# The logits products of a part in two portions of 24, in a mixture-of-experts kernel

## The chip, the cores and the metric

The kernel runs on one core of a Trainium2 chip. A core has five engines that work side by side: TensorE (PE, matrix products; its weight loads are listed apart as PEld), VectorE (DVE), ScalarE (ACT), GpSimd (POOL) and SyncE (SP, which here only issues transfers). Each works through its own instructions in order. TensorE writes its results to PSUM, a small memory of 8 banks, from which VectorE and ScalarE fetch them; all else is held in SBUF.

The metric is the device time of one execution in microseconds, lower being better. A profile is one more execution, recorded instruction by instruction.

## What is computed

A short convolution along the sequence, then a layer of eight experts, of which each token uses one. The reference, cut to what matters:

```python
B, S, D, E, F = 8, 3584, 192, 8, 1024          # everything in float32

# convolution: 8 heads of 24 channels, 7 taps each, softmax over the taps
out = np.einsum('hk,bskhg->bshg', w, x_unf)

# experts
logits = np.einsum('bsd,de->bse', x, w_gate)
local_gate = 1.0 / (1.0 + np.exp(-np.einsum('bsd,de->bse', x, w_local).squeeze(-1)))
for b in range(B):
    prev_e = -1
    for s in range(S):
        fresh_e = int(np.argmax(logits[b, s]))
        if s == 0 or local_gate[b, s] < 0.5:
            e = fresh_e
        else:
            e = prev_e if prev_e >= 0 else fresh_e
        prev_e = e
        ls = logits[b, s] - logits[b, s].max()
        p = np.exp(ls)
        p /= p.sum() + 1e-09
        h = np.maximum(x[b, s] @ w1[e], 0.0)
        out[b, s] = p[e] * (h @ w2[e])
```

A token takes the expert with the largest logit, or, if its local gate is open, the expert of the token before it. The eight logits and the local gate of a token are nine products over 192 channels. They are small beside the two products with w1 and w2, but nothing of a token's expert is known before them.

## The kernel before

The 28,672 tokens are cut into 16 parts of 1792. A part goes through three stages.

- *Convolution.* In the first two parts it is done as products of TensorE (`wide`). In the other 14, `conv` does it: the first tap of a head on ScalarE (L378), six more on VectorE (L388).
- *Route.* `route` (L603) finds each token's expert and its place among that expert's tokens. It begins with `logits` (L566): VectorE transposes the part in squares of 32 by 32 into the tile z (L572); TensorE forms the logits (L582); ScalarE copies them out of PSUM (L587, tile ls); VectorE transposes them back (L590, lq) and puts them in order (L598, lt). Some hundred short VectorE operations follow; they end in the places of the tokens (posi, L747) and in tables of which rows and whose weights a block needs (L847). `put` (L770) has GpSimd scatter the rows to their places in a DRAM buffer, slots.
- *Experts.* A block is one unit (n = 1) or two units (n = 2) of 128 tokens of one expert. SyncE loads its weights (wb, L906) and rows (xg, L913) ahead of time. For each block TensorE does three things: `hidden` (L952) forms the 1024 hidden values in two halves, `for two in range(2)`, of twelve products each (L963), and ScalarE applies relu (L968); `turn` (L930) transposes the rows of the block that comes next (L360, into the PSUM tile xps, then copied to xT by L947 and L949); `output` (L973) forms the result (L980, 16 products for each unit), which ScalarE (L988) and VectorE (L992) scale and add, and GpSimd scatters to the output (L996).

After the start, 55 blocks of one unit and 87 blocks of two are run: 35 of one unit, the 87 of two, then 20 of one. The convolution and the route of the later parts are worked into the first 96 of them.

The order of all instructions is the order in which the program writes them. `conv` and `route` are generators that give a time for each operation, and `step(time)` (L1037) takes operations from them until that time is used up: from the route first, from the convolution after. A route yields "hop" where it has to wait for another engine; then the rest of that call of `step` goes to the convolution, and the route goes on in the next call. `step` is called between turn and output (L1150), within output before line 992 (L990), and after output (L1152). The products of `logits` thus land where the call of `step` stands that reaches them.

The logits products are short. z holds four groups of tokens that lie on different rows, and the weights of the gate have 32 columns, so that one product uses 64 rows and 32 columns of TensorE and streams 128 values: six blocks of 32 channels, by four groups j, by two halves of the rows make 48 products. In float32, each appears in the profile as two products with a weight load each. The long products beside them (L963, L980) use 64 rows and all 128 columns.

PSUM holds one tile xps (two banks), four tiles hps, of which a half of `hidden` takes two, and two tiles yps, which an output takes. The sums of the logits are two of the hps tiles (L577).

Of the kernel before, what the change touches and what calls it, by code (L numbers as in the profile page):

```python
# [8 lines left out]
F32 = mybir.dt.float32  # L9
# [8 lines left out]
P = 128  # L18
# [19 lines left out]
BT = 2 * UT  # L38
# [25 lines left out]
Q = 32  # L64
DQ = D // Q
TQ = (NT + 3) // 4
# [15 lines left out]
def kernel(  # L82
# [10 lines left out]
    nc = tc.nc  # L93
# [11 lines left out]
    xps_p = ctx.enter_context(tc.tile_pool(name="xps_p", bufs=1, space=PSUM))  # L105
    hps_p = ctx.enter_context(tc.tile_pool(name="hps_p", bufs=4, space=PSUM))
# [77 lines left out]
    wgb, wgq = wg[:, :3, :], wg[:, 3:, :]  # L184
# [5 lines left out]
    def z_tile():  # L190
        return yt.tile([P, 3 * NH * TB + NB * DR], F32, name="z")
# [119 lines left out]
    rows = cst.tile([Q, 2, Q], F32, name="rows")  # L311
# [42 lines left out]
    def halves():  # L354
        return [(half, slice(half * DR, (half + 1) * DR)) for half in range(2)]
# [210 lines left out]
    def logits(g, y_sb):  # L566

        nc.gpsimd.tensor_copy(y_sb[:, :, Y0 + D:IX], y_sb[:, :, Y0 + P:Y0 + D])  # L568
        z = z_tile()[:, :NT * D].rearrange("p (t d) -> p t d", d=D)
        for t in range(0, NT, TQ):  # L570
            u = min(t + TQ, NT)
            nc.vector.transpose(z[:, t:u, :], y_sb[:, t:u, Y0:Y0 + D])  # L572
            yield 0.2 * (u - t)
        yield "hop"


        lps = [hps_p.tile([P, TQ * Q], F32, name="hps") for half in range(2)]  # L577
        begin = [min(TQ * j, NT - TQ) for j in range(4)]
        for b in range(DQ):
            for j in range(4):  # L580
                for half, rows in halves():
                    nc.tensor.matmul(lps[half][Q * j:Q * j + Q, :], lhsT=wgq[rows, b, :],  # L582
                                     rhs=z[rows, begin[j]:begin[j] + TQ, b * Q:(b + 1) * Q],
                                     start=(b == 0), stop=(b == DQ - 1))
        ls = sm.tile([P, 2, TQ * Q], F32, name="ls", bufs=1)
        for half in range(2):
            nc.scalar.copy(ls[:, half, :], lps[half])  # L587
        yield "hop"
        lq = sm.tile([P, 2 * TQ, Q], F32, name="lq", bufs=1)
        nc.vector.transpose(lq.rearrange("p t e -> p (t e)"), ls.rearrange("p h x -> p (h x)"))  # L590
        yield 0.4
        lt = sm.tile([P, NT + 2, E + 1], F32, name="lt")
        for r in range(4):
            for j in range(4):
                t, u = TQ * j, min(TQ * (j + 1), NT)
                at = r // 2 * TQ + t - begin[j]
                e0 = r % 2 * (E + 1)
                nc.vector.tensor_copy(lt[Q * r:Q * r + Q, t:u, :],  # L598
                                      lq[Q * j:Q * j + Q, at:at + u - t, e0:e0 + E + 1])
                yield 0.12  # L600
        return lt
# [168 lines left out]
    def put(behind=None):  # L770


        if not to_put:
            return
        g, rows, to = to_put.pop(0)
        nc.gpsimd.nop()
        ins = nc.gpsimd.indirect_dma_start(  # L777
            out=slots[:, :], in_=rows, in_offset=None,
            out_offset=bass.IndirectOffsetOnAxis(ap=to, axis=0)).ins
        if behind is not None:  # L780
            tc.add_manual_dep(ins, behind.ins.name, SYNC, reason="scatters apart")
        if puts:
            tc.declare_no_dep(ins, group="puts", reason="slots of their own")
        if g:
            tc.declare_no_dep(ins, group="gets", reason="those slots were full before")
        puts.append((g, ins))
        tc.add_to_no_dep_group("puts", ins)
        tc.add_to_no_dep_group(f"puts{g}", ins)
# [163 lines left out]
    def hidden(n, wb, xT, shares=(1, 1)):  # L952
        hT = hp.tile([P, FK, BT], F32, name="hT")
        w = slice(0, n * P)


        for two in range(2):
            hps = [hps_p.tile([P, 2, BT], F32, name="hps") for half in range(2)]
            for d in range(KD):
                for j in range(2):  # L960
                    f0 = (d * 4 + two * 2 + j) * P
                    for half, rows in halves():
                        nc.tensor.matmul(hps[half][:, j, w], lhsT=wb[rows, f0:f0 + P],  # L963
                                         rhs=xT[rows, d, w], start=(d == 0 and j == 0),
                                         stop=(d == KD - 1), skip_group_check=True)
            for half in range(2):
                m = half * 4 + two * 2
                relu = nc.scalar.activation(hT[:, m:m + 2, w], hps[half][:, :, w], Act.Relu)  # L968
            for _ in range(shares[two]):
                put(relu)  # L970
        return hT

    def output(n, wb, xg, hT):  # L973

        yps = [yps_p.tile([P, 512], F32, name="yps") for half in range(2)]
        for m4 in ([0, 1, 4, 5], [2, 3, 6, 7]):
            for k in range(n):
                for m in m4:
                    for half, rows in halves():
                        nc.tensor.matmul(yps[half][:, k * D:(k + 1) * D],  # L980
                                         lhsT=hT[rows, m, k * P:(k + 1) * P],
                                         rhs=wb[rows, WA + m * D:WA + (m + 1) * D],
                                         start=(m == 0 and k == 0), stop=(m == FK - 1),
                                         skip_group_check=True)
        o_sb = op.tile([P, KT, D], F32, name="o_sb")
        y = [[yps[half][:, k * D:(k + 1) * D] for half in range(2)] for k in range(n)]
        for k in range(n):
            nc.scalar.activation(o_sb[:, k, :], y[k][0], Act.Copy, scale=xg[:, k, 0:1])  # L988

        step(1.2)  # L990
        for k in range(n):
            nc.vector.scalar_tensor_tensor(o_sb[:, k, :], y[k][1], xg[:, k, 0:1], o_sb[:, k, :],  # L992
                                           Alu.mult, Alu.add)

            nc.gpsimd.nop()
            sent = nc.gpsimd.indirect_dma_start(  # L996
                out=out, in_=o_sb[:, k, :], in_offset=None,
                out_offset=bass.IndirectOffsetOnAxis(ap=xg.bitcast(I32)[:, k, IX:], axis=0),
                bounds_check=N - 1, oob_is_err=False)
            tc.declare_no_dep(sent.ins, group="sent", reason="each token has one slot")  # L1000
            tc.add_to_no_dep_group("sent", sent.ins)
# [1 line left out]

    LEAD = 2
    LATE = 3
    st = {"block": 0, "conv": 1, "cgen": None, "route": 1, "rgen": None, "routed": 1}

    def start_conv():
        g = st["conv"] + 1

        free = not any(p[0] <= g - 3 for p in to_put)
        if (st["cgen"] is None and g < NPART and g <= st["route"] + LEAD and free
                and (g != 3 or g in x_in and st["block"] > LATE + 2)):
            st["conv"] = g
            st["cgen"] = conv(g, x_in.pop(g))
            next(st["cgen"])
# [7 lines left out]
    def start_route():  # L1024
        done = st["conv"] - (st["cgen"] is not None)
        if st["rgen"] is None and st["route"] < done:
            st["route"] += 1
            st["rgen"] = route(st["route"])
# [8 lines left out]
    def step(time):  # L1037

        start_route()
        start_conv()  # L1040
        go = st["rgen"] is not None
        while time > 0:
            c = route_op() if go else conv_op()
            if c is None:
                if not go:
                    break
                go = False
            elif c == "hop":
                go = False
            elif c == "placed":  # L1050
                pass
            else:
                time -= c
# [85 lines left out]
    for i, (_, n, _, _) in enumerate(blocks):  # L1139
        st["block"] = i  # L1140
        ensure(i)
        weights(i + AHEAD)
        if i == LATE:
            x_in[3] = load_x(3)
        hT = hidden(n, wbs[i], xT, (1, 1) if i else (0, 0))
        if i + 1 < len(blocks):
            xT, copied = turn(blocks[i + 1][1], xgs[i + 1])
            if len(to_put) > NT // 2 and n == KT:
                put(copied)
        step(2.1 if n == 1 else 4.2)  # L1150
        output(n, wbs.pop(i), xgs.pop(i), hT)
        step(1.3 if n == 1 else 3.0)  # L1152

# [79 lines left out]
```

## Time and profile before

| | us |
|---|---|
| median of three runs | 1340.1 |
| lowest and highest | 1337.61 and 1342.41 |
| the profiled execution's own time | 1340.85 |
| its span, from the first to the last instruction | 1339.1 |

Groups of instructions of one line (busy time, and mean duration of one):

| line | engine | what | count | busy us | mean ns |
|---|---|---|---|---|---|
| L980 | PE | output products | 7328 | 647.0 | 326 |
| L963 | PE | hidden products | 6816 | 634.5 | 336 |
| L360 | PE | transposes of the rows | 916 | 60.3 | 221 |
| L388 | DVE | convolution | 672 | 376.1 | 569 |
| L968 | ACT | relu | 568 | 262.1 | 512 |
| L587 | ACT | copies of the logits | 28 | 6.1 | 269 |

Products on TensorE overlap, so that a group's busy time is less than its count by its mean. "Idle time before", where a line of a profile gives it, is the time for which that engine had nothing to do just ahead of these instructions, and the name behind the arrow is what ended it; "issue" is written where the engine waited for nothing that the profile shows. In an order of time, the columns are the start, the length, the engine and the line, the operation, what is written and read, and the number of instructions, with the idle time before them in brackets. In a table by stretches, each row is a stretch of the span: its length, each engine's busy time with the number of instructions, the clock granted to TensorE, the share of the DMA engines, and GB/s.

### The profile page before, as it was taken

The page shows a single profiled execution, that of the slowest core. Times are in us where ns is not written, and L with a number is a line of the kernel's source. Part 1 is how long each engine was busy: PE and PEld are TensorE (multiplying, and loading weights), DVE is VectorE, ACT ScalarE, POOL GpSimd, SP SyncE. Part 2 cuts the span into 40 slices and gives each one's busy share as a digit, 9 for nine tenths or more (in the row PEclk, how much of TensorE's full clock was granted, in tenths as well). Part 3 has the DMA queues.
Part 4 walks back from the last instruction along what each step waited for, and adds up shares of the span by engine and source line. Part 5 has one row for each costly group of instructions (what it writes and reads, how often), then busy time and mean ns, then how long its engine had stood idle before and what let it go on. Part 6 is the DMA issues. An engine that isn't in the chain of part 4 may idle for free. (4 is left out here: it accounts for less than half of the span.)

```text
span 1339.1 us, 41274 instructions
## 1 busy us (share of the span) xinstructions
PE 1315.2 (98%) x16682; PEld 1264.3 (94%) x16682; DVE 778.6 (58%) x2434; ACT 583.9 (44%) x1431; POOL 492.8 (37%) x538
## 2 busy tenths in 40 slices
PE   8899999999999999999999999999999999999997
PEld 7898999899999999999999999999999999999997
DVE  5878887877777777868786878786520000000000
ACT  5244544444444444444444444444334333334443
POOL 4455443534343434343434343434344211121111
PEclk9899999999999999999999999999999999999999
DMA  4799999977575857675767675756566655556893
GB/s 180 262 357 406 376 352 356 365 281 276 192 287 189 295 197 286 209 274 208 274 209 274 208 281 207 288 204 234 206 234 230 207 185 184 190 192 235 322 332 124
DMA packets 67298, 340.36 MB, mean 254 GB/s; under 512 B 12576, under 2 KB 23191, under 8 KB 47650
## 3 DMA queue, kind: packets, MB, share of 16 engines
q1 hardware_dynamic: 44784, 284.88, 59.2%
q0 software_dynamic: 22320, 52.82, 10.4%
q8 instruction: 133, 2.18, 0.6%
q14 instruction: 59, 0.48, 0.1%
q10 hardware_dynamic: 2, 0.00, 0.0%
HBM read 284.73 MB, written 53.41 MB: 253 GB/s over the span
## 5 line engine op out<-in xcount | busy, mean ns | idle before, releaser
L980 PE MATMUL yps<-wb,hT 64*128 64x192 f32 x7328 | 647.0, 326 | 8.2 <-ACT hT L968 5.3
L963 PE MATMUL hps<-xT,wb 64*128 64x256 f32 (+1 forms) x6816 | 634.5, 336 | 1.6 <-issue 1.2
L980 PEld LDWEIGHTS yps<-wb,hT 64*128 64x128 f32 x7328 | 603.7, 187 | 19.6 <-ACT hT L968 10.8
L963 PEld LDWEIGHTS hps<-xT,wb 64*128 64x128 f32 x6816 | 585.1, 187 | 28.7 <-issue 3.2
L996 POOL DMA_INDIRECT out_dram<-o_sb,xg x229 | 232.4, 1015 | 608.6 <-DVE o_sb L992 540.1
L968 ACT ACTIVATE hT<-hps 128x512 f32<-128x512 f32 (+1 forms) x568 | 262.1, 512 | 393.1 <-PE hps L963 271.6
L388 DVE SCALAR_TENSOR_TENSOR y_sb<-x_sb,c,y_sb 128x336 f32<-128x336 f32 x672 | 376.1, 569 | 20.1 <-ACT y_sb L378 2.0
L992 DVE SCALAR_TENSOR_TENSOR o_sb<-yps,xg,o_sb 128x192 f32<-128x192 f32 x229 | 87.5, 413 | 475.7 <-ACT o_sb L988 468.5
L777 POOL DMA_INDIRECT slots<-y_sb,posi x228 | 228.0, 1000 | 207.4 <-ACT hT L968 81.6
L988 ACT ACTIVATE o_sb<-yps,xg 128x192 f32<-128x192 f32 x229 | 86.9, 418 | 305.4 <-PE yps L980 299.7
L949 ACT COPY xT<-xps 64x256 f32<-64x256 f32 (+1 forms) x284 | 92.4, 325 | 7.0
L947 ACT COPY xT<-xps 128x512 f32<-128x512 f32 (+1 forms) x142 | 72.2, 509 | 5.9 <-PE xps L360 2.9
L360 PEld LDWEIGHTS xps<-ident,xg 64*128 64x128 f32 x916 | 60.2, 139 | 5.2
L378 ACT ACTIVATE y_sb<-x_sb,c 128x336 f32<-128x336 f32 x112 | 63.7, 581 | 1.0
L360 PE MATMUL xps<-ident,xg 64*128 64x64 f32 x916 | 60.3, 221 | 0.0
L572 DVE STREAM_TRANSPOSE z<-y_sb 128x768 f32<-128x768 f32 (+1 forms) x56 | 45.4, 852 | 0.4
L598 DVE COPY lt<-lq 32x36 f32<-32x36 f32 x224 | 41.0, 183 | 3.5
L582 PE MATMUL hps<-z,wg 64*32 64x128 f32 x1344 | 24.1, 272 | 0.7 <-issue 0.5
L582 PEld LDWEIGHTS hps<-z,wg 64*32 64x32 f32 x1344 | 19.0, 105 | 3.1 <-issue 2.3
L556 PE MATMUL yps<-y_sb 112*128 112x194 f32 x64 | 13.8, 377 | 1.8 <-DVE y_sb L550 1.8
L556 PEld LDWEIGHTS yps<-y_sb 112*128 112x128 f32 x64 | 12.5, 220 | 2.6 <-DVE y_sb L550 2.0
L568 POOL COPY y_sb<-y_sb 128x896 f32<-128x896 f32 x14 | 13.4, 954 | 0.0
(240 smaller groups left out, 384.0 us busy)
## 6 DMA issues: line engine op xcount, KB each, us to landing
wb<-in_w_dram SPq DMA_DIRECT2D x138, 1536.0 KB
x_sb<-in_x_dram SPq DMA_DIRECT2D x14, 1920.0 KB
xg<-slots SPq DMA_DIRECT2D x87, 259.0 KB
xg<-slots SPq DMA_DIRECT2D x53, 129.5 KB
wb<-in_w_dram SPq DMA_DIRECT2D x12, 512.0 KB
out_dram<-o_sb,xg POOLq DMA_INDIRECT x229
slots<-y_sb,posi POOLq DMA_INDIRECT x228
x_sb<-in_xb_dram SPq DMA_DIRECT2D x4, 768.0 KB
```

Source lines behind the costliest of these rows:

```text
L360: nc.tensor.transpose(to, src[rows], identity=ident[rows, rows])
L378: nc.scalar.activation(cols(h), chans(h, 0), Act.Copy, scale=c[:, h, 0:1])
L388: nc.vector.scalar_tensor_tensor(cols(h), chans(h, k), c[:, h, k:k + 1], cols(h), Alu.mult, Alu.add)
L777: ins = nc.gpsimd.indirect_dma_start(out=slots[:, :], in_=rows, in_offset=None, out_offset=bass.IndirectOffsetOnAxis(ap=to, axis=0)).ins
L947: nc.scalar.copy(first, by)
L949: copied = nc.scalar.copy(to[rows, :, 2], at[(DR, 0)[half]:(P, DR)[half], :, 0])
L963: nc.tensor.matmul(hps[half][:, j, w], lhsT=wb[rows, f0:f0 + P], rhs=xT[rows, d, w], start=(d == 0 and j == 0), stop=(d == KD - 1), skip_g ...
L968: relu = nc.scalar.activation(hT[:, m:m + 2, w], hps[half][:, :, w], Act.Relu)
L980: nc.tensor.matmul(yps[half][:, k * D:(k + 1) * D], lhsT=hT[rows, m, k * P:(k + 1) * P], rhs=wb[rows, WA + m * D:WA + (m + 1) * D], start= ...
L988: nc.scalar.activation(o_sb[:, k, :], y[k][0], Act.Copy, scale=xg[:, k, 0:1])
L992: nc.vector.scalar_tensor_tensor(o_sb[:, k, :], y[k][1], xg[:, k, 0:1], o_sb[:, k, :], Alu.mult, Alu.add)
L996: sent = nc.gpsimd.indirect_dma_start(out=out, in_=o_sb[:, k, :], in_offset=None, out_offset=bass.IndirectOffsetOnAxis(ap=xg.bitcast(I32)[ ...
```

## The change

The loop over the six blocks of 32 channels is cut into two portions of three, 24 products each, and the copies to ls follow the second. How the portions are kept apart depends on which call of `step` reaches them. A new flag, "ahead", is set during the call between turn and output.

- With the flag set, the sums are two hps tiles as before, now asked for with the full 512 columns of a bank. The first portion is written; a "hop" leaves it to the next call, which is the one within output, behind all products of line 980, to write the second portion and the copies; another "hop" follows.
- Without it, the sums are the two banks of an xps tile. The first portion is written where the step stands, behind an output. The second is left in st["amid"], and `hidden` of the next block calls it after its first half: behind the relus and puts of that half, ahead of the other twelve products.

In the order of instructions, 11 of the 14 parts have a whole output between the portions (16 products of line 980 in one part, 32 in ten), and three parts (the first, the second and the fourth) have the twelve products of line 963, after which twelve more follow. The number of products and copies is the same in both kernels.

```diff
-        lps = [hps_p.tile([P, TQ * Q], F32, name="hps") for half in range(2)]
+        if st["ahead"]:
+            lps = [hps_p.tile([P, 2 * BT], F32, name="hps") for half in range(2)]
+        else:
+            both = xps_p.tile([P, 2, 512], F32, name="xps")
+            lps = [both[:, half, :] for half in range(2)]
+        lps = [a[:, :TQ * Q] for a in lps]
         begin = [min(TQ * j, NT - TQ) for j in range(4)]
-        for b in range(DQ):
-            for j in range(4):
-                for half, rows in halves():
-                    nc.tensor.matmul(lps[half][Q * j:Q * j + Q, :], lhsT=wgq[rows, b, :],
-                                     rhs=z[rows, begin[j]:begin[j] + TQ, b * Q:(b + 1) * Q],
-                                     start=(b == 0), stop=(b == DQ - 1))
+
+        def products(bs):
+            for b in bs:
+                for j in range(4):
+                    for half, rows in halves():
+                        nc.tensor.matmul(lps[half][Q * j:Q * j + Q, :], lhsT=wgq[rows, b, :],
+                                         rhs=z[rows, begin[j]:begin[j] + TQ, b * Q:(b + 1) * Q],
+                                         start=(b == 0), stop=(b == DQ - 1))
+
         ls = sm.tile([P, 2, TQ * Q], F32, name="ls", bufs=1)
-        for half in range(2):
-            nc.scalar.copy(ls[:, half, :], lps[half])
-        yield "hop"
+
+        def others():
+            products(range(DQ // 2, DQ))
+            for half in range(2):
+                nc.scalar.copy(ls[:, half, :], lps[half])
+
+        products(range(DQ // 2))
+        if st["ahead"]:
+            yield "hop"
+            others()
+            yield "hop"
+        else:
+            st["amid"] = others
+            while st["amid"]:
+                yield "hop"
...
             for _ in range(shares[two]):
                 put(relu)
+            if st["amid"]:
+                st["amid"]()
+                st["amid"] = None
         return hT
...
+        st["ahead"] = True
         step(2.1 if n == 1 else 4.2)
+        st["ahead"] = False
```

## The prediction

> **What bounds the kernel now.** I read the page first, then the waits, then the order of time on TensorE around one part's logits.
>
> ```profile
> span 1339.1 us, 41274 instructions
> PE 1315.2 (98%) x16682; PEld 1264.3 (94%) x16682; DVE 778.6 (58%) x2434; ACT 583.9 (44%) x1431; POOL 492.8 (37%) x538
> q8 instruction: 133, 2.18, 0.6%
> L980 PEld LDWEIGHTS yps<-wb,hT 64*128 64x128 f32 x7328 | 603.7, 187 | 19.6 <-ACT hT L968 10.8 <-issue 8.2
> L582 PE MATMUL hps<-z,wg 64*32 64x128 f32 x1344 | 24.1, 272 | 0.7 <-issue 0.5
> L582 PEld LDWEIGHTS hps<-z,wg 64*32 64x32 f32 x1344 | 19.0, 105 | 3.1 <-issue 2.3
> ```
>
> TensorE is the bound from end to end: 98% busy, its clock granted in full (0.994 on average). So the change is worth what it adds to or takes from TensorE's own stream; VectorE (58%) and ScalarE (44%) count only where TensorE waits for them. The logits of line 582 are 1344 records: 14 parts of 48 products, each product two records with a weight load each, so 192 instructions in a burst. The third line tells how code arrives: 133 packets for 33,364 TensorE instructions, about one per 250. A burst eats most of a packet at once.
>
> ```profile
> 409.25 1.32 PEld L582 LDWEIGHTS hps<-z,wg 64*32 64x32 f32 x96
> 410.77 0.64 PEld L980 LDWEIGHTS yps<-wb,hT 64*128 64x128 f32 x6 [0.20 <-issue]
> 411.81 0.65 PEld L980 LDWEIGHTS yps<-wb,hT 64*128 64x128 f32 x8 [0.41 <-issue]
> ```
>
> This is the order of time of the weight loads in the part at 409 us. The first row: 96 loads in 1.32 us. The second: 0.20 us of idleness where the products change from 32 columns back to 128; from the last logits record to the next one it is 0.20 in 13 of the 14 bursts and 0.51 in the other. The third: 1.24 us behind the last logits load, 0.41 us more with nothing that the profile shows being waited for. Such a second stall follows some bursts only.
>
> ```profile
> 403.55:416.50 12.95, 12.84 (x220) 12.22 (x218) 9.71 (x23) 5.97 (x14) 4.17 (x4) 1.00 0.52 180
> 416.50:427.28 10.78, 10.78 (x123) 10.74 (x122) 9.46 (x36) 4.70 (x10) 4.08 (x4) 1.00 0.55 191
> ```
>
> These are two blocks of two units, in stretches from one first product of line 963 to the next: with logits (first) and without. I took this period for every block off the trace. Of 77 two-unit blocks without logits nearly all last 10.68 us. The ten with logits last 12.34, 12.34, 12.46, 12.48, 12.66, 12.67, 12.83, 12.88, 12.95 and 13.06. So a burst costs 1.66 us where nothing stalls and up to 2.38 where something does.
>
> **The change, part by part.** No arithmetic changes: 48 products and two copies a part stay, in the same shapes. What moves is where the second 24 stand.
>
> *One more way in and out of the 32-column products.* Eight of the 96 records run at once, a round of eight starting every 0.110 us: 12 rounds are 1.32 us. The clean burst costs 1.66, so entering and leaving take 0.34 together; behind an output (the part at 270.8: 0.25 in, 0.20 out, from 1.78 us between the neighbours the usual 0.155 taken off) it is 1.62, so 0.30. Every part now pays it twice. The entry amid line 963's products (three parts) is in no row; the nearest rows are these. Lower bound: the idle 0.20 less a usual step of 0.06, so 0.14; upper bound: the longest exit, 0.51 at 344 us, less the same step, so 0.45. I take 0.30, since both places with a row give 0.30 to 0.34: 14 x 0.30 = **+4.2 us** (2.0 to 6.3).
>
> *Stalls behind and inside the bursts.* Over the clean 12.34 the ten blocks above add 0.12 + 0.14 + 0.32 + 0.33 + 0.49 + 0.54 + 0.61 + 0.72 = 3.3 us. In the four earlier parts the weight loads idle on "issue" for 0.43 (at 91.5), 0.33 (153.8) and 0.33 + 0.58 + 0.59 (212 to 215): 2.3 us. Beside many of them a code packet starts or lands within some tenths of a microsecond (starts at 344.24 and 412.00 for the stalls at 344.3, 345.3 and 411.8), while in the 77 blocks without logits only two stalls of this kind stand out (0.38 and 0.64 us at 315 and 591). So I read them as code that comes too slowly for 192 instructions in 1.3 us. Half a burst eats 96, and in 11 parts a whole output (64 records over 5.3 us) follows before the next 96, in which the supply can catch up. Bounds: all 5.6 us come back; or none does, if a half burst meets a packet's border as badly as a whole one; or it is worse by up to 0.3 us a part (the mean of the ten excesses), +4.2, if every half has its own stall. I take half, since the drain halves but the number of bursts doubles: **-2.8 us**.
>
> A page of the Trainium skill speaks against any gain here: "Runtime: NRT & Kernel Launch", section "Instruction fetch mechanics", has code streamed in 16 KiB blocks, with the crossing of a border mostly hidden because instructions are dispatched more slowly than they are filled in. By it nothing would be won, and the sum would be the 4.2 us of loss less the 0.4 below, 1344.7; the row at 411.81 (0.41 us idle, nothing waited for) is why I go by the half. "TensorEngine Tiling (Array Packing)", section "Key Properties", adds that a change of tiling mode, not of the tile, drains TensorE; it gives no price, and the row's 0.20 us is one.
>
> *PSUM.* Where the step stands between turn and output (11 parts), the two hps tiles are now held through the output. The next block's first half of line 963 takes the other two, its second half needs these: at least 1.3 us later (half of a one-unit block's 2.6), while the copies of line 587 take 0.27 us each. Cost nothing, cover about 0.8 us. In the other three parts the sums go to xps; the next turn needs it after twelve products (1.3 or 2.5 us), the copies need 0.5: hidden too. There the hps wait goes: "PEld hps L963 <- ACT ls L587" was 0.4 us in all, **-0.4 us**.
>
> *The steps of the route.* One more hop moves the rest of a part's route by one call of step, and what is left of that call goes to the convolution. Counting VectorE's order by the line-992 operations before it, the transpose of line 590 comes up to two later, but posi (line 747) and the tables (line 847) stand where they stood in every part but one, where posi is one later. SP's order changes in one place (a load of x_sb behind one more xg), POOL's in one (one copy of line 568 behind two scatters). VectorE is 9.7 us busy of 12.95 in the stretch above, so a late transpose has cover; without it a route would be late by about an output, 5 us, and only the loads of a new group of blocks would feel it.
>
> ```profile
> DVE lq L590 <- ACT ls L587: 12.2, 4, 6.1
> PEld yps L980 <- ACT hT L968: 10.8, 18, 0.8
> ```
>
> These are from the list of waits. The first mostly goes (the route is no longer called right behind its own products); it is not on TensorE's path, so it is worth nothing. The second I can't carry over exactly: 17 early one-unit blocks last 6.04 us rather than 5.45, since the third relu of line 968 starts 1.6 us behind the hidden products rather than 0.3. These blocks come in three spells, each begun near a stall of the same "issue" kind (105 and 110, 178, 240 us) and over by the next logits. Moving instructions may lengthen or shorten spells; at 0.59 us a block, up to eight blocks either way is about 5 us, with no sign that I can give. I take 0.
>
> **Sum.** +4.2 - 2.8 - 0.4 = +1.0 us on the profiled execution's 1340.85 (span 1339.1 and 1.75 around it): 1341.9. That execution is 0.75 above the median of 1340.1; against the median the sum is 1341.1, and I say **1341.5 us**, between the two.
>
> **Rivals.** *Slower: each half burst has its own stall.* The place is the output (or the second half of hidden) behind the first portion and the block behind the second. For it: the 0.20 us exit stands behind bursts of any part, even where no packet is near. Against: the two clean bursts at 867 and 933 us, with none. Price: 4.2 for the ways in and out less 0.4, nothing recovered, and 0 to 4.2 of new stalls: 1344.7 to 1348.9, say 1346. It decides from the point where less than about 0.6 us of the stalls is recovered.
>
> *Faster: the stalls go, and with them spells of late relus.* For it: the spells begin behind stalls, and all 5.6 us of the parts' stalls are of a kind that a shorter burst should ease. Against: the stalls that begin the spells stand away from the logits. Price: +4.2 - 5.6 - 0.4 and eight blocks of 0.59: -6.5, so 1334.
>
> *The change doesn't split at all.* If the second call came at once, the records would stand together as before, 1340. The order of instructions shows 24 and 24 with 32, 16 or 12 products between in all 14 parts, so I give it nothing.
>
> **How the numbers follow.** Within 0.3% of 1340.1 is 1336.1 to 1344.1, about what a measurement of this kernel can tell from no change. The forecast case, partial recovery and spells about as now, has 0.42 and gives 1336 to 1344 by itself; the slower rival 0.36; the faster one 0.22. The range takes in most of both rivals: 1334.5 to 1347.5, leaving about 1 in 10 out on either side.
>
> **What would show it.** Two-unit blocks that hold a first or second portion: 10.68 + 0.66 + 0.30 = 11.64 us each, or 12.3 together where both fall into one period; the ten parts' total over plain blocks was 19.9 us, and with half of the stalls left I expect 16.6 + 3.0 + 1.6 = 21.2; the sum is wrong if it is under 19.9 or over 23. The weight loads should show 0.20 us behind both portions, 28 times in place of 14, and fewer second stalls of 0.3 to 0.6 in line 980. The early one-unit blocks at 6.04 us should be 17 give or take eight. I would be wrong through them, or if a wait on ls, xps or hps appears in front of line 963 or 360.

## The result, and the profile after

| | before | after |
|---|---|---|
| median, same chip | 1339.1 (4 runs, 1337.61 to 1342.41) | 1340.31 (4 runs, 1338.03 to 1341.14) |
| ratio of the two, 95% interval | | 1.0003 (0.9979 to 1.0026) |
| the profiled execution's own time | 1340.85 | 1340.45 |
| its span | 1339.1 | 1338.7 |

No difference that can be measured: the interval allows 2.8 us less to 3.5 us more. 1341.5 us had been predicted. The page of the changed kernel, in the lines that answer to those of before (line 582 is now 591, line 980 is 1005):

```profile
span 1338.7 us, 41275 instructions
PE 1312.7 (98%) x16682; PEld 1243.5 (93%) x16682; DVE 781.1 (58%) x2434; ACT 582.8 (44%) x1431; POOL 490.5 (37%) x538
q8 instruction: 133, 2.18, 0.6%
L1005 PEld LDWEIGHTS yps<-wb,hT 64*128 64x128 f32 x7328 | 596.9, 188 | 22.6 <-ACT hT L990 14.1
L591 PEld LDWEIGHTS hps<-z,wg 64*32 64x32 f32 x1056 | 14.9, 105 | 4.1 <-issue 3.4
```

TensorE is as full as before. Line 591 has 1056 records here, 11 parts of 96; the other three parts write to xps and form a row of their own. The page can't say whether two effects cancel or none was there. The order of the weight loads in the part at 407 us can:

```profile
407.46 0.67 PEld L591 LDWEIGHTS hps<-z,wg 64*32 64x32 f32 x48
408.33 5.18 PEld L1005 LDWEIGHTS yps<-wb,hT 64*128 64x128 f32 x64 [0.20 <-issue]
413.73 0.67 PEld L591 LDWEIGHTS hps<-z,wg 64*32 64x32 f32 x48 [0.23 <-issue]
414.60 0.95 PEld L985 LDWEIGHTS hps<-xT,wb 64*128 64x128 f32 x10 [0.20 <-ACT o_sb L1013]
```

Two portions of 48 loads, 0.67 us each, 0.20 us of idleness behind each, and an output of 64 loads between them in one piece: the second stall of 0.41 us that this part had before is gone. The last line names ScalarE as what ended the idle time, but that 0.20 is as long as the others; the work named had been done, so I take the idleness for that of the change of shape. By stretches, from one first hidden product to the next (length; busy time of PE, PEld, DVE, ACT and POOL; clock; DMA share; GB/s):

```profile
401.94:414.60 12.66, 12.66 (x219) 11.47 (x216) 9.51 (x18) 6.36 (x14) 4.16 (x4) 1.00 0.53 184
414.60:425.39 10.79, 10.79 (x126) 10.21 (x123) 9.92 (x42) 4.30 (x10) 3.90 (x4) 1.00 0.55 191
425.39:436.07 10.68, 10.68 (x124) 10.08 (x123) 9.15 (x47) 4.30 (x10) 3.89 (x4) 1.00 0.53 193
```

A block with both portions, the block behind it, a plain block. Taken off the trace for all ten such parts: before 12.34 to 13.06 us, and behind them 10.68 (10.79 and 10.81 in two parts); after 12.66 in eight parts and 12.84 in two, and 10.78 behind each. So the loss and the recovery are both there: the dear blocks became cheaper, the cheap ones dearer. From the first plain two-unit block to the end of the last, 939.7 us became 940.7; blocks 2 to 35 ahead of them, one-unit blocks but for the last, took 216.6 and now 216.1; the rest is the start of the program, 0.9 us shorter, which the change doesn't touch.

### The profile page after: what moved, and what is told of

The parts are those of the page before. It is cut to its first block, busy times and chain, and to the rows that moved or that the text cites. A ratio compares the mean times of both kernels' runs of the same rounds, so it can differ in the third digit from the quotient of the medians.

```text
span 1338.7 us, 41275 instructions
## 1 busy us (share of the span) xinstructions
PE 1312.7 (98%) x16682; PEld 1243.5 (93%) x16682; DVE 781.1 (58%) x2434; ACT 582.8 (44%) x1431; POOL 490.5 (37%) x538
## 5 line engine op out<-in xcount | busy, mean ns | idle before, releaser
L1005 PE MATMUL yps<-wb,hT 64*128 64x192 f32 x7328 | 639.9, 326 | 11.6 <-ACT hT L990 7.7
L985 PE MATMUL hps<-xT,wb 64*128 64x256 f32 (+1 forms) x6816 | 626.5, 336 | 1.2 <-DVE at L480 1.2
L1005 PEld LDWEIGHTS yps<-wb,hT 64*128 64x128 f32 x7328 | 596.9, 188 | 22.6 <-ACT hT L990 14.1
L985 PEld LDWEIGHTS hps<-xT,wb 64*128 64x128 f32 x6816 | 563.8, 187 | 41.4 <-ACT o_sb L1013 2.0
L360 PEld LDWEIGHTS xps<-ident,xg 64*128 64x128 f32 x916 | 52.1, 138 | 7.5
L360 PE MATMUL xps<-ident,xg 64*128 64x64 f32 x916 | 53.4, 221 | 0.0
L591 PE MATMUL hps<-z,wg 64*32 64x128 f32 x1056 | 21.4, 275 | 0.3 <-issue 0.3
L591 PEld LDWEIGHTS hps<-z,wg 64*32 64x32 f32 x1056 | 14.9, 105 | 4.1 <-issue 3.4
```

Of the source, the lines that this page charges most:

```text
L360: nc.tensor.transpose(to, src[rows], identity=ident[rows, rows])
L1005: nc.tensor.matmul(yps[half][:, k * D:(k + 1) * D], lhsT=hT[rows, m, k * P:(k + 1) * P], rhs=wb[rows, WA + m * D:WA + (m + 1) * D], start= ...
```

## The experiments

The runs were made in three groups of four, each group on one chip, and the chips are of two kinds. Where the result above was taken, and for e5 to e8, the kernel before takes 1339 us; for e1 to e4 and for e9 to e12 it takes 1320. So each run is compared with the kernel before on its own chip, and the kind of chip is part of what was measured. "First kind" and "second kind" below mean these. What makes the difference between them, no run shows.

**Whole burst, other place (e1).** The changed kernel, but all 48 products behind the output in the 11 parts that are reached ahead of one:

```diff
+        first = 0 if st["ahead"] else DQ // 2
...
-        products(range(DQ // 2))
+        products(range(first))
```

> In the eleven parts whose step stands between turn and output, all 48 products now follow the output in one go; the other three parts are as in the changed kernel. Theory A (the stalls behind a whole burst come from the speed at which 192 instructions are drawn, wherever they stand): the ten two-unit parts again cost unequal amounts over a plain block of 10.68 us, 1.6 to 2.4, about 20 us in all as before the change, with idle weight loads of 0.3 us or more behind some bursts. Theory B (what matters is the place: the short instructions of an output right behind the burst, rather than its length): the ten parts cost 1.62 to 1.77 each, 16 to 18 us in all, with no second stall, some 3 to 4 us less than the changed kernel's 21.3.

1319.49 us in one run, the kernel before 1320.03 (13 runs). The ten blocks last 12.40 to 12.43, the blocks behind them 10.78. By the ten blocks alone (17.4 us over plain ones) that is what theory B asked for, and there is almost no stall: a gap of about 0.11 us before the last load of a burst, or behind it. But it decides nothing between the two: the same kernel on a chip of the first kind (e7) reads quite differently.

**Three portions (e2).** Where the changed kernel writes 24 and 24 around the output, 16 ahead of it, 16 in its middle, 16 behind:

```diff
-        products(range(DQ // 2))
+        products(range(2 if ahead else DQ // 2))
...
+            st["within"] = lambda: products(range(2, 4))
...
```

> In the same eleven parts three portions of 16 products: ahead of the output, amid it, and behind it. Theory A (each way in and out of the 32-column products has a fixed price, 0.42 us in the changed kernel where the prediction took 0.30): the ten two-unit parts cost 2.09 + 0.4 = 2.5 us each over plain blocks, 25 us in all, and the kernel is 4 us slower than the changed one. Rival (the price is that of a long burst's supply and shrinks with the portion): 21 to 22 us in all, as in the changed kernel.

1323.63 us, 3.6 over the kernel before; the ten blocks 12.91 or 12.92, the blocks behind 10.79. Together with e10 (two portions, 12.66 and 10.78) and e9 (one portion ahead of the output, 12.34 and 10.68 in most parts) this prices the ways in and out on chips of the second kind. Nothing stalls in these parts, and over plain blocks of 10.68 a part costs 1.66 us with one portion, 2.08 with two, 2.34 with three. So the way behind the output is worth 0.42 us, and the one amid it 0.26: theory A asked for 0.4, the rival for nothing. The one burst behind the output in e1 costs 1.82 to 1.85; that is more than the 1.66 ahead of it by the 0.11 us of stall and by 0.05 to 0.08 for the place.

**Scatters later, second kind of chip (e3).** The kernel before with both scatters of a block behind its last relu:

```diff
-        hT = hidden(n, wbs[i], xT, (1, 1) if i else (0, 0))
+        hT = hidden(n, wbs[i], xT, (0, 2) if i else (0, 0))
```

> The kernel before, with both scatters of a block behind the relus of the second half of hidden, where one stood behind each half. It is to tell what makes the third relu late in the early one-unit blocks. In both profiles a scatter starts on GpSimd about 0.14 us after the last hidden product in each of these blocks and in none of the punctual ones. Theory P (that scatter holds up the semaphore of the hidden products): with it moved away, the 17 blocks of 6.04 us last 5.45, and the kernel takes about 10 us less, 1330. Rival C (the convolution's work on VectorE and ScalarE, which runs in the same blocks, does it): the blocks still last 6.04, 1340.

1320.51 us (10 runs), ratio 1.0003 (0.9993 to 1.0012). Inconclusive: e1 and e2 keep the scatters where they were and have no late third relu on this chip either, so there was nothing to cure.

**The burst doubled (e4).** The kernel before, every logits product made twice:

```diff
-        for b in range(DQ):
+        for b in [*range(DQ), *range(DQ)]:
```

> The kernel before, with every part's 48 logits products done twice in one go (the second pass starts the sums anew, so the sums stay the same). Theory A (code comes too slowly for a burst): 384 instructions in 2.6 us cross at least one packet's border, so gaps of 0.3 us or more stand inside or behind nearly all of the 14 bursts, and the ten two-unit parts cost more than 1.32 us beyond their 20 us, that is over 3.3 us each on average, 35 to 40 in all. Rival (no such limit; the stalls are of the place): 1.32 us more each, 33 us in all.

1364.23 us, 44.2 over the kernel before. The 48 products more take 1.32 us a part, 18.5 in 14 parts; nearly all of the other 25.7 are stalls. The ten blocks cost 44.7 us over plain ones, where theory A asked for 35 to 40 and the rival for 33. One burst, weight loads and scatters in the order of time:

```profile
411.41 1.71 PEld L582 LDWEIGHTS hps<-z,wg 64*32 64x32 f32 x113
412.63 0.96 POOL L777 DMA_INDIRECT slots<-y_sb,posi  x1 [1.50 <-DMA wb<-in_w_dram]
413.27 0.10 PEld L582 LDWEIGHTS hps<-z,wg 64*32 64x32 f32 x1 [0.15 <-issue]
414.55 1.09 PEld L582 LDWEIGHTS hps<-z,wg 64*32 64x32 f32 x78 [1.17 <-issue]
415.83 0.79 PEld L980 LDWEIGHTS yps<-wb,hT 64*128 64x128 f32 x10 [0.20 <-issue]
```

113 loads run with no gap over 0.1 us, although a scatter begins 1.22 us behind the first; then comes a stall of 1.17 us. Counted in groups of 256 from the program's start (143 packets brought the 36,366 TensorE instructions that the trace has, about 254 each), the load that waits is number 193, and a code packet landed 1.26 us before it started. All nine stalls of over 1 us within these bursts are at number 193, and end 1.3 to 1.6 us behind a packet's landing. So I read them as late code packets; what the instruction waits for, the trace doesn't name. In a normal burst they are rare: in the kernel before one of the ten parts has such a stall (0.52 us at 678.7).

**Both kernels on a chip of the first kind (e5, e6).** No edit.

> The kernel before once more, to have its trace on the same chip as the next runs (ratio 1.000). The last chip was 20 us faster than the first and showed no late third relu and only small stalls. Theory S (the stalls behind the burst of 96 records are code that comes too slowly, and how slowly differs by chip): on a chip of the first kind the ten two-unit logits blocks spread from 12.3 to 13.1 us and 15 to 20 early one-unit blocks last 6.04; on a chip of the second kind the ten blocks last 12.40 to 12.53 and all early one-unit blocks 5.45.

> Theory S: the half bursts never stall, so the ten two-unit logits blocks last 12.66 us and the block behind each 10.78, on any chip; against the kernel before that is +1 us on a chip of the first kind (3.3 us of stalls there), and +3 to +4 us, ratio 1.002 to 1.003, on one of the second kind (1 us of stalls there). Rival (the ways in and out cost no more than 0.30 and half of the stalls stay): 12.6 to 12.9 with a spread between the parts, ratio 1.000 to 1.001 on either chip.

The kernel before: 1339.24 us (12 runs), ratio 1.0003 (0.9994 to 1.0012). The changed one: 1342.90 (6 runs, 1341.02 to 1343.98), ratio 1.0034 (1.0021 to 1.0046). So on this chip the change is a little slower; the first interval, up to 1.0026, doesn't exclude the same there. The ten blocks: 125.5 us together before (12.34 to 12.53 and one of 13.72), 127.0 after (12.66 to 12.69, two of 12.84), and 1.0 more in the blocks behind. That is 2.5 of the difference; the profiled executions (1340.76 and 1341.02) hide it behind a start of the program that was 2.5 us shorter in the second.

**Whole burst behind the output, first kind of chip (e7).** The kernel of e1.

> All 48 products in one go behind the output in 11 parts. Theory S: one way in and out as in the kernel before, so the ratio is 0.999 to 1.000 on a chip of the second kind; on one of the first kind the bursts stall here too (the ten blocks spread over 0.3 us or more). Rival (it is the place ahead of the output that makes the stalls, not the length of the burst): no spread on either chip, 12.40 in all ten blocks, and 2 to 3 us under the kernel before on a chip of the first kind.

1360.56 us (5 runs), ratio 1.0162 (1.0145 to 1.0179): 22 us slower, where nothing was seen on the other kind. The ten blocks last 12.96 in one part and 14.10 to 14.47 in nine. Theory S had stalls here, but none of such a size, and the rival had none. One such burst, with GpSimd's scatters:

```profile
483.22 1.23 PEld L593 LDWEIGHTS hps<-z,wg 64*32 64x32 f32 x84 [0.23 <-PE yps L1007]
484.29 0.99 POOL L1023 DMA_INDIRECT out_dram<-o_sb,xg  x1 [3.89 <-DVE o_sb L1019]
484.89 0.13 PEld L593 LDWEIGHTS hps<-z,wg 64*32 64x32 f32 x3 [0.44 <-issue]
485.58 0.99 POOL L1023 DMA_INDIRECT out_dram<-o_sb,xg  x1 [0.30 <-issue]
485.62 0.19 PEld L593 LDWEIGHTS hps<-z,wg 64*32 64x32 f32 x5 [0.59 <-issue]
486.38 0.15 PEld L593 LDWEIGHTS hps<-z,wg 64*32 64x32 f32 x4 [0.58 <-issue]
486.73 0.80 PEld L987 LDWEIGHTS hps<-xT,wb 64*128 64x128 f32 x6 [0.20 <-issue]
```

The burst runs freely for 84 loads. At 484.29 GpSimd begins the scatter of the output, and 0.16 us later TensorE stands idle: 0.44 us, three loads, 0.59 us, five loads, 0.58 us, four loads. That goes on until the burst is through. No code packet stands beside it. In e1 the same burst and scatter stand thus:

```profile
461.21 1.52 PEld L593 LDWEIGHTS hps<-z,wg 64*32 64x32 f32 x96 [0.23 <-issue]
462.46 0.99 POOL L1023 DMA_INDIRECT out_dram<-o_sb,xg  x1 [4.33 <-DVE o_sb L1019]
462.85 1.38 PEld L987 LDWEIGHTS hps<-xT,wb 64*128 64x128 f32 x14
```

The scatter begins 0.18 us later against the burst (1.25 instead of 1.07), when 95 of 96 loads have started. That is not all of the difference: in e4, on the same chip as e1, the doubled burst at 480 us has a whole scatter in its second half and loses 0.4 us in all.

**Scatters later, first kind of chip (e8).** The kernel of e3; its TensorE instructions are those of the kernel before, in the same order.

> The kernel before with both scatters of a block behind the last relu rather than one behind each pair. Theory P (the third relu is late where a scatter of GpSimd starts at the end of the hidden products): where the kernel before has 15 to 20 late blocks, this has none or few and is 8 to 11 us faster, ratio 0.992 to 0.994; where it has none, no difference. Rival C (the late relus come from the stalls of code and have nothing to do with the scatters): as many late blocks as the kernel before on the same chip, ratio 1.000.

1357.68 us (4 runs), ratio 1.0144 (1.0126 to 1.0161). The expectation failed by its sign, for two reasons that the trace keeps apart. The late relus did go: one-unit blocks with a third relu over 1 us late fell from 20 (e5) to 3, and blocks 2 to 35 from 218.6 us to 214.6, though the four logits blocks among them grew by 5.6. But the ten two-unit logits blocks went from 125.5 us to 145.7. In the same order, first e8 and then e5, for the part at the same place:

```profile
405.94 1.24 PEld L582 LDWEIGHTS hps<-z,wg 64*32 64x32 f32 x86
407.03 0.97 POOL L777 DMA_INDIRECT slots<-y_sb,posi  x1 [3.11 <-DMA wb<-in_w_dram]
407.60 0.15 PEld L582 LDWEIGHTS hps<-z,wg 64*32 64x32 f32 x4 [0.41 <-issue]
408.30 0.96 POOL L777 DMA_INDIRECT slots<-y_sb,posi  x1 [0.30 <-issue]
408.35 0.13 PEld L582 LDWEIGHTS hps<-z,wg 64*32 64x32 f32 x3 [0.60 <-issue]
409.09 0.16 PEld L582 LDWEIGHTS hps<-z,wg 64*32 64x32 f32 x3 [0.61 <-issue]
```

```profile
409.51 1.32 PEld L582 LDWEIGHTS hps<-z,wg 64*32 64x32 f32 x96
411.03 2.09 PEld L980 LDWEIGHTS yps<-wb,hT 64*128 64x128 f32 x26 [0.20 <-issue]
411.07 1.07 POOL L777 DMA_INDIRECT slots<-y_sb,posi  x1 [1.83 <-DMA wb<-in_w_dram]
```

The first scatter behind the burst's first load begins 1.09 us after it in e8, with another behind it, and 1.56 us in e5. The same products, the same order on TensorE, the same chip: only the scatters' place differs, and with it 1.6 us of stalls. That the place decides is thus shown. What the next runs call theory G is a reading of it: while GpSimd issues a scatter, TensorE gets next to no new instructions, and a burst that has just used up what was fetched ahead stands still.

With that in hand the kernel before on the first chip can be read again. Its part at 409.25 us has this between burst and second stall (the stall ends at 411.81):

```profile
410.52 1.16 POOL L777 DMA_INDIRECT slots<-y_sb,posi  x1 [1.73 <-DMA wb<-in_w_dram]
```

The distance from a burst's first load to that scatter, for all ten parts, the length of the block, and how much of what it has over 12.34 comes from the burst's first load on:

```
kernel before, first chip                             kernel before, e5
1.27  13.06  0.54      1.34  12.48  0.01              1.38  12.53  0.00      1.58  12.36  0.02
1.28  12.95  0.43      1.40  12.46  0.00              1.42  12.53  0.00      1.60  12.38  0.04
1.29  12.83  0.31      1.43  12.34  0.00              1.44  12.52  0.00      1.60  12.38  0.04
1.32  12.66  0.14      1.45  12.88  0.50 (packet)     1.56  12.34  0.00      1.60  12.38  0.04
1.33  12.67  0.14      1.47  12.34  0.00              1.57  12.35  0.01      1.61  13.72  1.38 (packet)
```

The burst is over after 1.32 us. A scatter that begins 0.05 us before that costs 0.54 us, one that begins 0.02 us after it or later nothing to 0.04. The two parts marked have the other kind of stall, at number 193 and 1.3 to 1.5 us behind a code packet.

The rest of a block's excess stands ahead of its burst, which starts up to 0.19 us later: 5.70 us behind the block's first product in the part at 409.25, 5.51 in e5's at 409.51. There the weight loads are out of step. In most blocks two loads of line 963 start within 0.01 us of one another and the next two 0.22 us later; behind a stall the second of a pair comes up to 0.19 us late, in block after block, until a burst with no stall behind it ends that. In e5 this lasts from the stall at 315.9 us to the part at 343.8 and then begins again only at the stall at 590.2. So a stall is paid once more at the next part. Of the 3.3 us that the ten blocks of before had over the clean 12.34, 1.6 stand beside a scatter, 0.5 is a late packet, and 1.2 are brought along from stalls before.

**The scatter out of the way (e9).** The kernel before, with the second scatter of a two-unit block behind the copies of turn:

```diff
-        hT = hidden(n, wbs[i], xT, (1, 1) if i else (0, 0))
+        hT = hidden(n, wbs[i], xT, ((1, 1) if n == 1 else (1, 0)) if i else (0, 0))
...
+            if n == KT:
+                put(copied)
```

> The kernel before, with the second scatter of a two-unit block behind the copies of turn instead of behind its fourth relu, so about 1 us later, when the whole burst of 96 records is over. Theory G (TensorE gets next to no new instructions while GpSimd issues a scatter, and a whole burst has emptied what was fetched ahead): the ten two-unit logits blocks last 12.34 us each, no second stall, on any chip; 2 to 3 us (0.1 to 0.3%) under the kernel before on a chip of the first kind, 0.5 to 1 us on the other. Rival S (192 instructions in 1.3 us are too many for the code supply, whatever GpSimd does): the ten blocks spread as in the kernel before, 12.34 to 12.5 with single ones of 12.7 to 13.7.

On a chip of the second kind: 1319.44 us (11 runs), ratio 0.9994 (0.9981 to 1.0006). Eight of the ten blocks last 12.34 or 12.35, as theory G asks; in e3, with the scatter at 1.21 to 1.23 us, those eight had lasted 12.43 to 12.53. The ratio alone would show nothing. The other two are 13.77 and 12.53; the second starts its burst 0.18 us late, out of step since the stall of the first. The order at one of the eight, then at the part of 13.77:

```profile
389.57 1.32 PEld L582 LDWEIGHTS hps<-z,wg 64*32 64x32 f32 x96
391.10 2.58 PEld L980 LDWEIGHTS yps<-wb,hT 64*128 64x128 f32 x32 [0.20 <-issue]
392.05 0.96 POOL L777 DMA_INDIRECT slots<-y_sb,posi  x1 [2.76 <-ACT xT L949]
```

```profile
652.56 1.32 PEld L582 LDWEIGHTS hps<-z,wg 64*32 64x32 f32 x96
654.08 2.25 PEld L980 LDWEIGHTS yps<-wb,hT 64*128 64x128 f32 x26 [0.20 <-issue]
657.77 0.30 PEld L980 LDWEIGHTS yps<-wb,hT 64*128 64x128 f32 x4 [1.44 <-issue]
```

In the first, the scatter is 2.5 us behind the burst's start and nothing stalls. In the second, the stall of 1.44 us is at number 193 and 1.52 us behind a packet. It is the same instruction that waits in the kernel before (0.52 us), e5 (1.35), e9 and e12 (1.37); moving the scatter doesn't touch it. In the changed kernel, where half of the burst comes 5 us later, it doesn't occur.

**The changed kernel with the scatters later (e10).** The edit of e3, made to the changed kernel.

> The changed kernel with both scatters of a block behind the last relu. The same placement made the kernel before 19 us slower on a chip of the first kind, since the scatters fell into its bursts. Theory G: portions of 48 records do not empty what was fetched ahead, so the ten two-unit logits blocks stay at 12.66 (up to 12.9); what the early blocks gain from punctual relus (4 to 10 us) is left, so 1331 to 1337 us where the kernel before takes 1339 (ratio 0.994 to 0.998); 1322 to 1324 on a chip of the second kind. Rival S: a portion that meets a scatter stalls too, the ten blocks last 13 us and more, 1350 us.

The second kind of chip again: 1322.03 us (11 runs), ratio 1.0009 (1.0000 to 1.0018). All ten blocks are at 12.65 or 12.66. But the scatters begin 1.22 us behind a portion's first load, 0.55 behind its end, so this doesn't try a scatter that begins within a portion. What this kernel does on a chip of the first kind, for which it was made, wasn't tried.

**Put together (e11, e12).** Both have the scatters as in e9 for two-unit blocks and as in e3 for one-unit blocks. e11 is the changed kernel with whole bursts in two-unit blocks, e12 the kernel before:

```diff
+        hT = hidden(n, wbs[i], xT, ((0, 2) if n == 1 else (1, 0)) if i else (0, 0))
...
+        first = DQ if st["ahead"] and blocks[st["block"]][1] == KT else DQ // 2
+        products(range(first))
```

> Put together from the parts: the logits in two portions only where the blocks have one unit (4 parts of 14), in one go in the two-unit blocks; both scatters behind the last relu in one-unit blocks, the second one behind the copies of turn in two-unit blocks. Theory G: ten blocks of 12.34, few late relus: 1327 to 1332 us where the kernel before takes 1339 (ratio 0.991 to 0.995), 1319 to 1322 on a chip of the second kind. Rival S: the ten blocks spread as in the kernel before, 1331 to 1336.

> As the run before but with every burst in one go (the kernel before with the scatters alone moved). Theory G: the ten two-unit logits blocks at 12.34; the four early bursts meet scatters and lose 1 to 2.5 us each, so 1331 to 1336 us where the kernel before takes 1339, 3 to 6 us over the run with the early parts split. Rival S: the early bursts cost no more than in the kernel before, so it is within 2 us of the run with the early parts split.

1319.16 us, ratio 0.9989 (0.9980 to 0.9998), and 1318.65 us, ratio 0.9985 (0.9976 to 0.9994), both 11 runs on the second kind of chip. Both are under the kernel before by 1 to 1.5 us, within the 0.3% that the prediction took for what a measurement can tell; the ten blocks are at 12.34 but for the one with the late packet (13.45 and 13.69) and the one after (12.52 and 12.53). The larger gain expected of them is for chips of the first kind, and they weren't run on one.

## Why the prediction was right

In the ten two-unit parts, which can be added up, two terms were off in opposite directions, by 1.2 us each. That they cancel there is luck. At the same prices all 14 parts make 5.9 - 3.4 = +2.5 us, where +1.0 had been added up; an interval from 2.8 us less to 3.5 us more can't tell these apart.

*The way in and out was sized too low.* It was put at 0.30 us, 4.2 for 14 parts. The runs show 0.42 for the second portion behind an output: 1.66 for a part in one go (e9), 2.08 in two (e10, and 12.66 and 10.78 in the changed kernel on both kinds of chip). At that price 14 parts pay 5.9; the three parts with the second portion amid `hidden` weren't priced alone. What the working missed is in the trace: for the part at 270.8 us the interval was read between the neighbours of the burst, and the first pair of products behind it was left out. Behind a portion the second pair of line 985 starts 0.32 us after the first, where it is 0.22 elsewhere; that is the 0.10 by which the block behind is longer, and with it the 0.30 would have been 0.40. (Behind a portion ahead of an output it is 0.27 for 0.16; there the 0.34 has it, since it comes from a whole block.) The working's longest exit, 0.51 at 344 us, is that of the products; by the weight loads the exit there is 0.20 too, and the longest is the 0.59 at 214.6 that it counts among the stalls. Its upper bound of 0.45 rests on that, its 0.30 doesn't.

*The stalls were sized too low too, and read wrongly.* Half of 5.6 us was to come back. In the ten two-unit parts 2.9 of 3.3 came back (two blocks of 12.84 are left, whose 0.18 us each is brought along from stalls at 313 and 589 us, in blocks without logits), in the early parts about 0.5 of 2.3 (gaps of 0.30, 0.61, 0.32 and 0.60 remain). Together 3.4, against 2.8. The step that failed is "So I read them as code that comes too slowly for 192 instructions in 1.3 us", with the code packets beside the stalls as its evidence. What keeps TensorE waiting behind the ten bursts of before is, in all but one of those that stall, a GpSimd scatter that begins within 0.05 us of the burst's end; that the scatters' place decides is shown by e8 against e5. No run ties the packets near these stalls to them. In the ten parts of the changed kernel such a scatter begins 1.26 to 1.53 us behind a portion's first load, about 0.6 us or more behind its end, when TensorE is at the long products again, and nothing stalls. Whether a portion is spared because it leaves half of what was fetched ahead, as theory G has it, or because the scatter comes so late, isn't shown: whole bursts were spared too once the scatter came 0.02 us behind their end. And a portion isn't proof against a scatter: the one at 210.3 us, with a scatter from 0.25 us ahead of it, stalls for 0.32 and 0.60.

*The hps wait of 0.4 us* was two waits of 0.2, as long as the idleness behind every burst, and the same 0.20 stands behind the ten second portions with ScalarE's o_sb as its name. So I take it for the change of shape under another name, already in the first term: worth 0.

*Late relus* were taken as 0, give or take 5 us. Third relus over 1 us late: 24 blocks instead of 17. Blocks of over 5.9 us among the early ones without logits: 18 instead of 19. The stretch of blocks 2 to 35 is 0.5 us shorter: those that hold a portion took 0.9 more, the others 1.4 less. So 0, give or take 5, was right. What makes them is the next point that the prediction had wrong, which saw each spell "begun near a stall": e8 shows that the scatters' place decides, 20 against 3.

*The rest held.* The wait of line 590 for ls went from 12.2 us to 5.5, and no wait of TensorE came of it. From the first logits on, no wait on ls, xps or hps of any size stands before line 985 or 360. The 0.20 us is there behind all 28 portions.

*The sum that was to show it:* ten parts' total over plain blocks, 21.2 expected. Measured: 20.2 in the blocks with logits and 1.05 in those behind them, 21.2. It was expected as 16.6 + 3.0 + 1.6 and is 16.6 + 4.2 + 0.4. The single block was foretold wrongly, by a slip: 12.3 for both portions in one period, while 10.68 and twice 0.96 make 12.60; it is 12.66.

*The rivals.* "Each half burst has its own stall" fell: in the ten two-unit parts no portion has one, in the four early parts three of eight do. Its sign was right on the chip of e6, at 1342.9, but the way in and out did that. "The stalls go, and with them spells of late relus": the first half came true in the ten parts, the second didn't, and the dearer way took the gain.

*The rules of the Trainium skill.* "Runtime: NRT & Kernel Launch", section "Instruction fetch mechanics", has the crossing of a border mostly hidden. If the stalls at number 193 are borders, that holds in nine of the ten parts of e9, with 1.44 us in the tenth, and fails in nine of the fourteen doubled bursts of e4 (1.14 to 3.74 us; right behind two others there are 1.26 and 0.89). Its sum, 1344.7, was yet further off than the one taken, since most stalls were no borders.

## What to carry to other kernels

An idle time called "issue" behind a dense run of short TensorE instructions needs the whole order of time of all engines beside it, GpSimd's above all, not only TensorE's and the code packets': two runs with the same order on TensorE, whose first scatter behind the burst's start differs by 0.3 to 0.6 us, differ by 20 us in ten parts. Before a burst is split, price each further way in and out over the first instructions behind it as well (here 0.26 to 0.42 us), and see whether what collides with it can be moved at no price. And take the trace of before and after on one chip: what the change recovers here depends on the chip, what it costs doesn't.

## What the runs showed of the hardware

- *While a scatter is issued, a dense burst gets few instructions.* On a chip of the first kind whole bursts got three to five loads in each 0.75 us while scatters of 0.96 to 0.99 us were being issued (e7, e8), against eight in 0.11 us otherwise. On one of the second kind a burst lost 0.4 us under a whole one (e4). How a scatter does this, no run shows.
- *How soon it is felt.* In the ten two-unit parts of e7 and e8 the scatter begins after 80 to 95 of a burst's loads, and the first gap comes at most five loads later; in the early part of e8 at 264.8 us it begins after 16, and the gap comes 17 later. So little is left late in a burst. How much is fetched ahead can't be read from this, since no row shows what came in meanwhile.
- *A stall is paid twice.* Behind it the loads of a pair stay up to 0.19 us out of step, and the next burst starts up to 0.19 us later (the ten parts of before: 1.2 of 3.3 us).
- *Two kinds of chips.* The same kernel takes 1339 us on the one and 1320 on the other. Most of it is in the early one-unit blocks (blocks 2 to 35: 216.6 and 218.6 us against 200.9 in e3 and 201.6 in e9): the late third relus occur on the first kind alone. There, a scatter begins at about the end of the hidden products, and the third relu starts 1.6 us behind them. On the second kind a scatter begins as near in some blocks (0.12 to 0.15 us behind the last product in two of e1 and one of e9), and the relu comes after 0.1 to 0.3. In e5:

```profile
144.13 0.97 POOL L777 DMA_INDIRECT slots<-y_sb,posi  x1 [0.30 <-issue]
145.67 0.66 ACT L968 ACTIVATE hT<-hps 128x256 f32<-128x256 f32 x2 [1.99 <-PE xps L360]
```

The last hidden product of this block starts at 143.99; the scatter begins at 144.13, and ScalarE, with nothing else to do, starts the relu at 145.67, after the scatter's end. That the scatter holds back what TensorE has to report, as it holds back its instructions, would fit, but no run shows it.
